# A planned recurrence and feed-forward kernel on one core: later loads planned as late, and part of the first group's up products in split passes

## The chip, the cores and the metric

The kernel runs on one core of one Trainium2 chip. The metric is device time in microseconds (us) of one execution, the median over runs. TensorE multiplies matrices, VectorE, ScalarE and GpSimd do elementwise work, SyncE issues the transfers between DRAM and the on-chip memory. Each engine works through its own instructions strictly in order. An instruction whose operand is not ready holds back all that stand behind it on its engine.

## The reference

What is computed is a recurrence over 768 steps for 4 batches and 8 heads of width 48, and then a two-layer product over the 3072 tokens that it gives:

```python
for t in range(S):                                  # B=4, H=8, S=768, D=48
    cur = np.einsum('bhd,bhe->bhde', u[None] * kt, vt)
    y[:, :, t] = np.einsum('bhd,bhde->bhe', rt, state + cur)
    state = wt[:, :, :, None] * state + np.einsum('bhd,bhe->bhde', kt, vt)
...
h = x @ w_in                                        # x: y as 3072 x 384; w_in: 384 x 2048
g = np.maximum(h, 0.0) + alpha * np.minimum(h, 0.0)
return g @ w_out                                    # w_out: 2048 x 384
```

All is fp32.

## The kernel before

The time axis is cut into 12 blocks of 64 steps, and the batches into two pairs, so there are 24 *chunks* (q = 0 to 23) of 128 tokens. Each chunk is loaded by SyncE in three or four transfers (`load`: wd, kr, rk, nv) and prepared on VectorE, GpSimd and ScalarE (`prep`: two scans of the decays wd, two products that scale the keys and queries kr, a sum cd, eight small scalings into at). TensorE then makes its scores, its outputs and the new state St (`scores`, `outputs`, L452), and a transposition (L498).

Three chunks make a *group* (g = 0 to 7) of 384 tokens. A group goes through the 16 *tiles* (j = 0 to 15, called tile 1 to tile 16 here) of the hidden width. For each tile there is an *up* product (`moe_up`, L669) into a bank, then L674 on ScalarE and L676 on VectorE for the activation `pos`, and, two tiles later, the *down* products (`moe_down`, L694) that add into the three accumulators op0 to op2. The program's names in the profile and in the order's rows carry running numbers (wf_81 is the first tile of wf, wf_96 the sixteenth in the kernel before).

There are two ways to multiply. Groups 1 to 7 split each operand into a high part in fp32r and the remainder, also in fp32r (x, wh and wl, gh and gl), and do three fp32r passes: nine instructions of 384 columns for an up product. Group 0 multiplies the unsplit fp32 operands (x_0, named xw in the rows, and wf): three fp32 instructions for an up product, each of which shows as two rows of TensorE. The splitting of a weight tile is `weight_parts`: ScalarE casts wf to wh (L650) and VectorE subtracts (L651, wl). Ahead of it `weight_tile` rebuilds a tile of weights from its 64-bit packing: one ScalarE instruction (L630) and three on VectorE (L632, L635, L639), the last of which writes wf.

The order of all engines' instructions is fixed when the program is built. `Plan.order` plays a list of operations with assumed durations and waits, and picks on each engine the ready one with the earliest due time. The due times come from tables of constants (FIRST, PLACE, PLACE_REST, AHEAD, ATT). For a transfer it assumes a landing DMA_LAT + lat after the issue. Where it sees TensorE idle ahead of the first use of op2, it puts in *fillers* (L818), products that nobody reads. Late in the program the inputs are loaded once more to be checked on ScalarE (`check_load`, L766, ScalarE lines L774, L783 and L784).

Ahead of each of groups 1 to 7, once its third chunk's x is split (L574, L585), four transfers (L606) move parts of x into place; the group's first up product waits for them.

## Time and profile before

| | us |
|---|---|
| median of 3 runs | 511.61 (507.61 to 512.86) |
| the profiled execution | 509.13 |
| its span, first to last instruction | 507.3 |
| TensorE busy in it | 494.3 |
| VectorE busy | 338.2 |
| ScalarE busy | 290.8 |
| GpSimd busy | 79.4 |

The profiled execution is one run of its own: 1.8 us of its time lie outside the span. Busy times of TensorE count pipelined instructions up to their modelled ends, so that the time one takes from the engine is read from one start to the next.

### The profile page before, as it was taken

The page shows a single profiled execution, that of the slowest core. Times are in us where ns is not written, and L with a number is a line of the kernel's source. Part 1 is how long each engine was busy: PE and PEld are TensorE (multiplying, and loading weights), DVE is VectorE, ACT ScalarE, POOL GpSimd, SP SyncE. Part 2 cuts the span into 40 slices and gives each one's busy share as a digit, 9 for nine tenths or more (in the row PEclk, how much of TensorE's full clock was granted, in tenths as well). Part 3 has the DMA queues.
Part 4 walks back from the last instruction along what each step waited for, and adds up shares of the span by engine and source line. Part 5 has one row for each costly group of instructions (what it writes and reads, how often), then busy time and mean ns, then how long its engine had stood idle before and what let it go on. Part 6 is the DMA issues. An engine that isn't in the chain of part 4 may idle for free.

```text
span 507.3 us, 13038 instructions
## 1 busy us (share of the span) xinstructions
PE 494.3 (97%) x5404; PEld 457.8 (90%) x5404; DVE 338.2 (67%) x602; ACT 290.8 (57%) x746; POOL 79.4 (16%) x103
## 2 busy tenths in 40 slices
PE   8999998999999999999999999999999999999994
PEld 8976664699999999999998999989999999999994
DVE  7999999999886656938377474945566344343331
ACT  5866485453454536457584656667677676553331
POOL 2111333350114010402014020220000000000000
PEclk9999999999999999999999999999999999999998
DMA  8966776550352302735175653746455531210001
GB/s 311 365 212 228 265 238 213 151 161 23 111 149 79 112 22 77 221 90 202 49 216 163 159 175 105 237 131 205 147 179 159 170 127 63 88 42 6 1 3 53
DMA packets 27109, 72.42 MB, mean 143 GB/s; under 512 B 3680, under 2 KB 8224, under 8 KB 27040
## 3 DMA queue, kind: packets, MB, share of 16 engines
q1 hardware_dynamic: 26656, 71.19, 43.9%
q8 instruction: 44, 0.72, 0.6%
q10 hardware_dynamic: 384, 0.30, 0.2%
q14 instruction: 25, 0.20, 0.1%
HBM read 64.70 MB, written 4.72 MB: 137 GB/s over the span
## 4 chain that ended last, share of the span: by engine, by line
PE 78%; DVE 12%; DMA 5%; issue 2%; SPq 1%; ACT 1%; DVEq 0%; ACTq 0%
PE bank L669 35%; PE op L694 33%; PE bank L452 7%; DMA raw<-in_wts_dram 2%; DVE cx L635 2%; DVE wf L639 2%; DVE suf L395 2%; DMA kr<-in_dmaj_dram 1%; PE bank L498 1%; DVE pos L676 1%; DVE kr L404 1%; DVE kr L407 1%; DVE cx L632 1%; PE bank L561 1%; DVE wd L401 1%
## 5 line engine op out<-in xcount | busy, mean ns | idle before, releaser
L669 PE MATMUL bank<-x,wh 128*128 128x384 f32 x672 | 191.7, 339 | 0.5 <-DMA x<-x 0.5
L674 ACT ACTIVATE pos<-bank,alpha_n 128x384 f32<-128x384 f32 (+1 forms) x133 | 75.3, 567 | 100.7 <-PE bank L669 100.3
L676 DVE SCALAR_TENSOR_TENSOR pos<-bank,pos 128x384 f32<-128x384 f32 (+1 forms) x133 | 71.3, 536 | 82.3 <-ACT pos L674 82.1
L669 PEld LDWEIGHTS bank<-x,wh 128*128 128x128 f32 x672 | 123.0, 188 | 2.5 <-ACT os L711 1.1
L694 PE MATMUL op<-wh,gh 128*128 128x384 f32 x336 | 113.3, 337 | 0.8 <-ACT gh L680 0.8
L694 PE MATMUL op<-wh,gl 128*128 128x384 f32 x336 | 112.8, 336 | 1.4 <-DVE gl L681 1.2
L694 PE MATMUL op<-wl,gh 128*128 128x384 f32 x336 | 112.5, 335 | 0.0
L669 PE MATMUL bank<-x,wl 128*128 128x384 f32 x336 | 112.4, 335 | 0.0
L681 DVE TENSOR_TENSOR gl<-pos,gh 128x384 fp32r<-128x384 f32 x112 | 68.3, 610 | 55.6 <-ACT gh L680 54.9
L680 ACT CAST gh<-pos 128x384 fp32r<-128x384 f32 x112 | 57.4, 512 | 51.4 <-DVE pos L676 51.2
L694 PEld LDWEIGHTS op<-wh,gl 128*128 128x128 f32 x336 | 63.1, 188 | 2.5 <-DVE gl L681 2.5
L694 PEld LDWEIGHTS op<-wh,gh 128*128 128x128 f32 x336 | 63.1, 188 | 1.4 <-ACT gh L680 1.4
L669 PEld LDWEIGHTS bank<-x,wl 128*128 128x128 f32 x336 | 63.1, 188 | 0.1
L694 PEld LDWEIGHTS op<-wl,gh 128*128 128x128 f32 x336 | 63.1, 188 | 0.0
L443 POOL TENSOR_TENSOR St<-St,pc_all 128x192 f32<-128x192 f32 x44 | 25.1, 589 | 232.5 <-DVE St L596 172.1
L433 ACT ACTIVATE at<-twin,cd 128x64 f32<-128x64 f32 x192 | 52.9, 340 | 2.4 <-DVE cd L428 1.9
L425 POOL TENSOR_TENSOR rk<-rk,u_bc 128x384 f32<-128x384 f32 x19 | 24.3, 1279 | 93.2 <-DMA rk<-in_nat_dram 50.5
L669 PE MATMUL bank<-xw,wf 128*128 128x384 f32 (+2 forms) x126 | 35.3, 418 | 1.8 <-DVE wf L639 1.7
L694 PE MATMUL op<-wf,pos 128*128 128x384 f32 x96 | 34.4, 489 | 0.0
L395 DVE TENSOR_TENSOR_SCAN suf<-wd,low 128x528 f32<-128x528 f32 x24 | 30.0, 1248 | 3.7 <-DMA wd<-in_dmaj_dram 3.7
L669 PEld LDWEIGHTS bank<-xw,wf 128*128 128x128 f32 x126 | 20.6, 190 | 12.5 <-DVE wf L639 2.9
L401 DVE TENSOR_TENSOR_SCAN wd<-wd,low 128x528 f32<-128x528 f32 x24 | 31.6, 1318 | 0.1
(81 smaller groups left out, 530.5 us busy)
## 6 DMA issues: line engine op xcount, KB each, us to landing
raw<-in_wts_dram SPq DMA_DIRECT2D x32, 768.0 KB, 4.7
kr<-in_dmaj_dram SPq DMA_DIRECT2D x24, 512.0 KB, 4.0
rk<-in_nat_dram SPq DMA_DIRECT2D x19, 384.0 KB, 3.4
wd<-in_dmaj_dram SPq DMA_DIRECT2D x24, 264.0 KB, 2.9
raw<-in_dmaj_dram SPq DMA_DIRECT2D x12, 528.0 KB, 4.0
nv<-in_nat_dram SPq DMA_DIRECT2D x24, 256.0 KB, 4.9
out_dram<-os SPq DMA_DIRECT2D x44, 96.0 KB, 2.2
x<-x SPq DMA_DIRECT2D x28, 72.0 KB, 4.2
```

The lines of the kernel that those rows point to most:

```text
L395: op("DVE", 1.17, lambda: nc.vector.tensor_tensor_scan(out=suf.ap[:, ::-1], data0=w.ap[:, ::-1], data1=low[:, ::-1], initial=0.0, op0=ALU. ...
L401: op("DVE", 1.17, lambda: nc.vector.tensor_tensor_scan(out=w.ap, data0=w.ap, data1=low, initial=0.0, op0=ALU.mult, op1=ALU.max), r=["low"] ...
L425: op("POOL", 1.0, lambda i=i: nc.gpsimd.tensor_tensor(out=rk.ap[:, 0:HD], in0=rk.ap[:, 0:HD], in1=u_bc if i == 0 else rk.ap[:, HD:], op=AL ...
L433: nc.scalar.activation(out=at.ap[:, o, p, :], in_=twin, func=AF.Copy, scale=cd.ap[:, o * NP + p:o * NP + p + 1])
L443: op("POOL", 0.6, lambda i=i: nc.gpsimd.tensor_tensor(out=St[b][:, i, :, 0:D], in0=St[b][:, i, :, 0:D], in1=pc_all[:, q, i::2].unsqueeze(2 ...
L452: nc.tensor.matmul(yb[q][i].ap[rows, cols], start=(i, rows.start) not in opened[q], stop=stop, skip_group_check=True, **kw)
L669: nc.tensor.matmul(hp.ap[:, ts], lhsT=a, rhs=b[:, k, ts], start=(i == 0), stop=(i == m - 1))
L674: op("ACT", 0.15 + 0.33 * share, lambda: nc.scalar.activation(out=pos.ap[:, ts], in_=hp.ap[:, ts], func=AF.Relu, scale=alpha_n[:, j:j + 1] ...
L676: op("DVE", 0.07 + 0.4 * share, lambda: nc.vector.scalar_tensor_tensor(out=pos.ap[:, ts], in0=hp.ap[:, ts], scalar=0.0, in1=pos.ap[:, ts], ...
L680: op("ACT", 0.43, lambda: nc.scalar.copy(out=gh.ap, in_=pos.ap), r=[pos], w=[gh])
L681: op("DVE", 0.47, lambda: nc.vector.tensor_tensor(out=gl.ap, in0=pos.ap, in1=gh.ap.bitcast(F32), op=ALU.subtract), r=[pos, gh], w=[gl], lo ...
L694: nc.tensor.matmul(ops_[s], lhsT=a.ap[:, ts], rhs=w, start=(j == 0 and i == 0), stop=(j == NF - 1 and i == len(todo) - 1))
```

## The change

Seven things change; the reference's result is computed in both.

1. In the planner, a transfer marked `kind` counts as landed LATE = 4.6 later than before for those that read it. Marked are the loads of chunks 6 to 23 and all check loads.
2. With UPS = 10, the up products of group 0 from tile 11 on take the three fp32r passes. For them the three chunks of x_0 are split once more into a ring tile `parted` (one ScalarE copy, one VectorE subtraction for each chunk), and the first halves of tiles 11 to 16 are split at once when they are rebuilt.
3. The weight tiles are kept in halves (up half 0, down half 1): the last rebuilding step and the splitting are two instructions of 384 columns where one of 768 stood. The ring cx has two places in place of one.
4. JOIN = 6: chunks 4, 5 and 6 get their scores in an operation of their own, not joined to the chunk before.
5. The due times are new (FIRST, PLACE, PLACE_REST, EDGE, AHEAD 14.2, ATT 1.23).
6. The unused constant `minus` and the path LO_BY_PE go.
7. In groups 0 to 6 the middle accumulator is copied out by ScalarE, not by VectorE.

```diff
-ATT = 0.5
-JOIN = 3
-AHEAD = 8.8
+ATT = 1.23
+JOIN = 6
+AHEAD = 14.2
...
+LATE = 4.6
+LATE_FROM = 6
+UPS = 10
...
                     dma = max(dma, end + DMA_LAT) + o.lat
-                    end = dma
+                    end = dma + (LATE if o.kind else 0.0)
...
+        def w_low(j, i):
+            slot = j if i == 0 and j >= UPS else (j - 1) % (NF + 1)
+            return half(wl, j, i, slot, F32R)
...
-        r_cx = ring("cx", [P, 2 * DM], 1, I32)
+        r_cx = ring("cx", [P, 2 * DM], 2, I32)
...
-            natural = q >= U_BY_PE
-            op("SP", 0.4, lambda: nc.sync.dma_start(out=w.ap, in_=dmaj[q, :, 0:SC]), w=[w], lat=0.75)
+            natural, far = q >= U_BY_PE, q >= LATE_FROM
+            op("SP", 0.4, lambda: nc.sync.dma_start(out=w.ap, in_=dmaj[q, :, 0:SC]), w=[w], lat=0.75, kind=far)
...
+            if g == 0 and UPS < NF:
+                part = lambda l: parted.ap[:, l, 0:KT, ss]
+                op("ACT", 0.42, lambda: nc.scalar.copy(out=part(0), in_=x_0[:, :, ss]), ...
+                op("DVE", 0.47, lambda: nc.vector.tensor_tensor(
+                    out=part(1), in0=x_0[:, :, ss], in1=part(0).bitcast(F32), op=ALU.subtract), ...
...
-                op("DVE", 0.07 + 0.4 * n, lambda x=x, w0=w0, full=full: nc.vector.tensor_tensor(
-                    out=full().bitcast(I32), in0=x(), in1=w0(), op=ALU.add), r=[k0, cx], w=keys("wf"), lock=True,
-                   due=tile_due[j] - AHEAD)
+                for i in range(i0, i1):
+                    early = i == 0 and j >= UPS
+                    op("DVE", 0.47, lambda cx=cx, fi=fi, full=full: nc.vector.tensor_tensor(
+                        out=full().bitcast(I32), in0=cx.ap[:, fi], in1=raw.ap[:, fi, 0], op=ALU.add), ...
+                    if early:
+                        parting(j, i, full, [cx, (cx, i)])
+        def parting(j, i, full, source):
+            op("ACT", 0.41, lambda: nc.scalar.copy(out=wh[:, j, i, :], in_=full()), r=source, w=[("wh", j, i)])
+            op("DVE", 0.47, lambda: nc.vector.tensor_tensor(
+                out=w_low(j, i), in0=full(), in1=wh[:, j, i, :].bitcast(F32), op=ALU.subtract), ...
...
         def moe_up(n, g, s0, s1, j):
-            x = xs[g]
+            parts = g > 0 or j >= UPS
+            x = xs[g] if g > 0 else parted
...
-                if s == 1 or last and s == GS - 1:
+                if last and s > 0:
```

The table of due times sets the order anew on every engine. Three places matter for what follows. TensorE, near 14 us, after the scores of the first two chunks; L498 and L507 are transpositions, L561 and L571 spread a chunk's outputs, L418 and L427 make a chunk's sums, L818 and L832 are fillers. Before:

```order
L498 MATMUL bank_75<-ident,kr_119 128x112 x4
L818 MATMUL op_74<-os_144 128x128 x2
L561 MATMUL bank_78<-os_144,os_145 128x64 x3
L561 MATMUL bank_79<-os_144,os_145 128x64 x3
L818 MATMUL op_74<-os_144 128x128
```

After:

```order
L427 MATMUL bank_75<-u_dm,rk_138 128x2 x4
L571 MATMUL bank_78<-os_160,os_161 128x64 x3
L571 MATMUL bank_79<-os_160,os_161 128x64 x3
L507 MATMUL bank_75<-ident,kr_136 128x112 x4
L832 MATMUL op_74<-os_160 128x128 x5
```

There are five fillers where three stood, and the sums of chunk 2 (rk_138) have moved ahead of the spreading; over the whole program the fillers are 25 in place of 16.

VectorE, at the last tile of group 0; wf_96 and cx_132 to wl_0_111 are tile 16, x_131 and x_149 the remainder of group 1's x, bank_77 and so on the chunk's outputs. Before:

```order
L632 TENSOR_SCALAR cx_115<-raw_114 128x768
L651 TENSOR_TENSOR wl_1014<-wf_82,wh 128x768
L635 SCALAR_TENSOR_TENSOR cx_115<-raw_114,cx_115 128x768
L651 TENSOR_TENSOR wl_1019<-wf_83,wh 128x768
L639 ISA wf_96<-raw_114,cx_115 128x1536
L676 SCALAR_TENSOR_TENSOR pos_136<-bank_79,pos_136 128x384
L651 TENSOR_TENSOR wl_1096<-wf_84,wh 128x768
L395 SCALAR_TENSOR_TENSOR suf_126<-wd_117,low 128x528
L585 TENSOR_TENSOR x_131<-bank_77,x_131 128x4x64
L585 TENSOR_TENSOR x_131<-bank_78,x_131 128x4x64
```

After:

```order
L638 TENSOR_SCALAR cx_132<-raw_130 128x768
L658 TENSOR_TENSOR wl_0_109<-cx_131,wh 128x384
L641 SCALAR_TENSOR_TENSOR cx_132<-raw_130,cx_132 128x768
L658 TENSOR_TENSOR wl_1_1158<-wf_1_82,wh 128x384
L648 ISA cx_132<-raw_130,cx_132 128x768
L648 ISA wf_1_112<-raw_130,cx_132 128x768
L586 TENSOR_TENSOR x_149<-bank_75,x_149 128x4x64
L586 TENSOR_TENSOR x_149<-bank_78,x_149 128x4x64
L658 TENSOR_TENSOR wl_0_111<-cx_132,wh 128x384
```

The remainder of x of group 1's third chunk, which stood behind the last tile, stands ahead of its last piece now, and the tile ends with a subtraction (L658) that waits for a ScalarE copy.

VectorE, at chunk 17's keys (kr_120 before, kr_137 after), whose transfer the trace shows late. Before:

```order
L676 SCALAR_TENSOR_TENSOR pos_137<-bank_77,pos_137 128x384
L483 COPY_PREDICATED at_130<-mask,bank_78 128x256
L398 RECIPROCAL low<-suf_126 128x8
L428 TENSOR_REDUCE cd_128<-rk_122 128x8
L681 TENSOR_TENSOR gl_143<-pos_137,gh_140 128x384
L401 SCALAR_TENSOR_TENSOR wd_117<-wd_117,low 128x528
L404 TENSOR_TENSOR kr_120<-kr_120,suf_126 128x512
L676 SCALAR_TENSOR_TENSOR pos_135<-bank_79,pos_135 128x384
```

After:

```order
L413 TENSOR_TENSOR kr_136<-kr_136,suf_143 128x512
L416 TENSOR_TENSOR kr_136<-kr_136,wd_133 128x512
L695 TENSOR_TENSOR gl_159<-pos_151,gh_156 128x384
L404 SCALAR_TENSOR_TENSOR suf_143<-wd_134,low 128x528
L690 SCALAR_TENSOR_TENSOR pos_153<-bank_77,pos_153 128x384
L407 RECIPROCAL low<-suf_143 128x8
L437 TENSOR_REDUCE cd_144<-rk_138 128x8
L410 SCALAR_TENSOR_TENSOR wd_134<-wd_134,low 128x528
L695 TENSOR_TENSOR gl_157<-pos_153,gh_154 128x384
L690 SCALAR_TENSOR_TENSOR pos_152<-bank_79,pos_152 128x384
L413 TENSOR_TENSOR kr_137<-kr_137,suf_143 128x512
```

Ahead of the first product on the late keys (L404 before, L413 after) there stand two more activations (pos) and one more remainder (gl) that do not need them.

## Rows read from the trace of the kernel before

**Rows 1.** The page: busy time, then slices of 12.7 us (VectorE, granted clock).

```profile
PE 494.3 (97%) x5404; PEld 457.8 (90%) x5404; DVE 338.2 (67%) x602; ACT 290.8 (57%) x746; POOL 79.4 (16%) x103
...
DVE  7999999999886656938377474945566344343331
...
PEclk9999999999999999999999999999999999999998
```

**Rows 2.** Busy us of each engine (executed instructions), clock, DMA, in 76 to 96 us.

```profile
76.00:96.00 20.00, 18.29 (x181) 10.96 (x180) 20.00 (x29) 11.00 (x28) 6.35 (x6) 1.00 0.58 196
```

**Rows 3.** Waits of TensorE: line, releaser, us in total, times, longest.

```profile
PE bank L669 <- DVE wf L639: 1.7, 2, 1.0
```

**Rows 4.** TensorE timeline, end of the first group: start, us, instruction, idle before.

```profile
76.82 2.10 PE L669 MATMUL bank<-xw,wf 128*128 128x384 f32 x6
78.76 2.10 PE L694 MATMUL op<-wf,pos 128*128 128x384 f32 x6
81.59 2.20 PE L669 MATMUL bank<-xw,wf 128*128 128x384 f32 x6 [0.74 <-DVE wf L639]
83.63 2.74 PE L694 MATMUL op<-wf,pos 128*128 128x384 f32 x8
87.35 2.20 PE L669 MATMUL bank<-xw,wf 128*128 128x384 f32 x6 [0.97 <-DVE wf L639]
...
93.02 0.43 PE L452 MATMUL bank<-kr,St 64*64 64x64 f32 x16
...
93.84 2.20 PE L669 MATMUL bank<-xw,wf 128*128 128x384 f32 x6
95.88 4.03 PE L694 MATMUL op<-wf,pos 128*128 128x384 f32 x12
100.44 0.41 PE L669 MATMUL bank<-x,wh 128*128 128x384 f32 x1 [0.52 <-DMA x<-x]
```

**Rows 5.** The chain of work, second group: start, us, what.

```profile
116.99 1.56 PE bank L669 x9
```

**Rows 6.** TensorE timeline, the first fillers (L818) and what follows.

```profile
5.69 0.61 PE L818 MATMUL op<-os 128*128 128x128 f32 x4
6.14 0.95 PE L418 MATMUL bank<-u_dm,rk 128*128 128x2 f32 x8
```

**Rows 7.** VectorE timeline, 91 to 96 us: the first group's last weight tile, the second group's x.

```profile
91.22 0.94 DVE L639 CUSTOM_DVE_ANT_0 wf<-raw,cx 128x1536 uint16<-128x1536 uint16 x1
92.08 0.55 DVE L676 SCALAR_TENSOR_TENSOR pos<-bank,pos 128x384 f32<-128x384 f32 x1
92.55 1.29 DVE L651 TENSOR_TENSOR wl<-wf,wh 128x768 fp32r<-128x768 f32 x1
93.77 1.24 DVE L395 TENSOR_TENSOR_SCAN suf<-wd,low 128x528 f32<-128x528 f32 x1
94.94 0.72 DVE L585 TENSOR_TENSOR x<-bank,x 128x256 fp32r<-128x256 f32 x2
```

**Rows 8.** The chain of work at the two late transfers: issue, us to landing.

```profile
259.62 7.54 DMA kr<-in_dmaj_dram
...
325.15 6.71 DMA raw<-in_wts_dram
```

**Rows 9.** VectorE and ScalarE timelines: who waited for those two transfers.

```profile
267.18 0.69 DVE L404 TENSOR_TENSOR kr<-kr,suf 128x512 f32<-128x512 f32 x1 [2.24 <-DMA kr<-in_dmaj_dram]
...
331.88 0.54 ACT L783 ACTIVATE raw<-raw 128x384 f32<-128x384 f32 x1 [3.30 <-DMA raw<-in_wts_dram]
```

**Rows 10.** TensorE timeline at the same two places.

```profile
268.94 0.44 PE L694 MATMUL op<-wh,gh 128*128 128x384 f32 x1
270.61 0.44 PE L694 MATMUL op<-wh,gl 128*128 128x384 f32 x1 [1.23 <-DVE gl L681]
...
331.69 0.34 PE L694 MATMUL op<-wl,gh 128*128 128x384 f32 x1
332.88 0.44 PE L694 MATMUL op<-wh,gh 128*128 128x384 f32 x1 [0.85 <-ACT gh L680]
```

## What was predicted

> **What bounds the kernel now.** I read the page's slices first, then the busy times by stretch, then TensorE's waits and the timelines at the places that these name. TensorE is busy 494.3 us of a span of 507.3, and its granted clock reads 9 in every slice but the last [rows 1], so it runs at its upper level of 2.4 GHz and no part of the change has a lower clock to win back or much idleness to remove. Almost all of the time is work. VectorE shows 9 in the slices from 13 to 127 us and falls to 3 to 6 later. The start, that is the attention of the first chunks, the rebuilding of the weights and group 0, has two engines full at once: from 76 to 96 us VectorE is busy 20.00 us of 20, ScalarE only 11.00, and TensorE 18.29 [rows 2].
>
> TensorE's real gaps after the first microseconds are few. Twice an up product waits for the last rebuilding step of its weight tile, 1.7 us in all [rows 3]; the timeline shows them at 81.59 (0.74) and 87.35 (0.97), and one for the moved parts of x at 100.44 (0.52) [rows 4]. Later there are two, both behind a late transfer. A load of keys took 7.54 us from 259.62 on, a check load 6.71 us from 325.15 on [rows 8]. The first kept VectorE waiting 2.24 us, the second ScalarE 3.30 us [rows 9], although neither product was wanted soon: in the queues behind them stood activations that TensorE did want, and it went idle at 268.94 and 331.69 [rows 10].
>
> So the change can gain in two places: at those two late transfers, and in the first 100 us, where it takes work from TensorE but gives work to the engine that is full.
>
> **The change part by part.**
>
> *Later landings in the plan.* Nothing is added to any engine; the order moves. The plan of before had the keys land 2.0 + 1.5 = 3.5 us after the issue, at 263.1; VectorE asked for them at 267.18 - 2.24 = 264.94. With 4.6 us more the plan holds them back to 8.1 us, over the 7.54 of the row; for the check load it is 2.0 + 2.0 + 4.6 = 8.6 against 6.71. The new order does what that asks: two activations, two remainders and the two products of the chunk before now stand between that chunk's x and the late keys, where one activation and one remainder stood. Each of the two more counts 0.47 us (the step from 92.08 to 92.55 in [rows 7]), each product of 512 columns 0.63 by the same rate: 2.2 us, as much as the 2.24 of the wait. What goes is TensorE's lost time: 268.94 to 270.61 less one step of 0.17 (a ninth of the 1.56 in [rows 5]) is 1.50 us, 331.69 to 332.88 less the same is 1.02. Sum 2.5 us. What is late next is the preparation of the following chunk, which has several units of 3.1 us ahead of its use. Bounds: 2.5 us of gain, and 0 if another wait takes their place. I take 2.5, because both transfers were shorter than what is now planned.
>
> The Trainium skill would say there was nothing to plan for: "DMA: Bandwidth & Descriptors", section "Anatomy of one DMA — SWDGE (gpsimd) path", fits 2.0 us plus bytes over 436 per ns, an estimate of 3.2 us for the 512 KB of keys. They would have landed at 262.8, ahead of VectorE's question, this term would be 0 and the result 509.3. That fit is for the GpSimd path, and the row here shows 7.54; the measurement decides.
>
> *Up products in three passes.* Six tiles change. An fp32 up product takes 78.76 - 76.82 = 1.94 us of TensorE [rows 4], nine fp32r instructions take 1.56 [rows 5]: 6 x 0.38 = 2.3 us less work.
>
> *Separate scores.* Chunks 4, 5 and 6 leave and enter the attention once more each. The up product behind attention takes 95.88 - 93.84 = 2.04 us, 0.10 more than the 1.94 without. I take as much again on the way in and inside, so 0.3 per chunk as an estimate, 0.9 in all, with 0.3 and 0.9 as ends.
>
> *Fillers.* Nine more. Two of them take 6.14 - 5.69 = 0.45 us [rows 6], so nine take 2.0. Where TensorE would stand idle they cost nothing; where it is late they cost all. They lie before 35 us. Ends 0 and 2.0.
>
> *VectorE until tile 16.* This is where the change adds. Counted in the two orders up to the last piece of tile 16:
> - The 16 rebuilding steps L639 (0.86, from 91.22 to 92.08 [rows 7]) become 32 of 384 columns (0.47): +1.3 us.
> - Three subtractions of 768 columns (0.86 like those) become four of 384, and six early ones are added: 10 x 0.47 - 3 x 0.86 = +2.1.
> - The remainders of x_0 for three chunks: +1.4.
> - One more sum (0.45) and two more remainders of x (0.66, from the row at 94.94): +1.1.
> - Chunk 6's preparation, two scans of 1.17 (93.77 to 94.94) and two products of 512 columns (0.63 each), moves behind: -3.6.
>
> Sum: +2.3 us. The last tile was ready at 92.08; it is ready at 94.4 then, and its up product starts there rather than at 93.84. Then 1.56 for it and 1.94 for three downs: 97.9. But group 1 also needs its x. Its remainder stands just ahead of the last piece, so at about 93.9, and from there the trace took 100.44 - 95.66 = 4.8 us for issuing and landing the moves: 98.7. At 100.44 the old order had one down left of group 0, the new one has three (2 x 0.67 more) and chunk 6's scores to do (93.02 to 93.84, 0.8). So 98.7 + 1.3 + 0.8 = 100.8 against 100.44: **+0.4 us**. The 2.3 us less of TensorE are used up in waiting for VectorE.
>
> The other end is a TensorE that waits for nothing: -2.3 (passes), -2.2 (the three waits of [rows 4]), +0.9 (scores), and fillers at 0 to 2.0, that is -3.6 to -1.6. I take +0.4, because VectorE had no idle time at all there [rows 2].
>
> The Trainium skill has a rule that speaks against halves: "Perfetto Trace Analysis", section "Optimizing Scalar/DVE Operations", puts an overhead of about 60 ns on each VectorE instruction on SBUF and advises larger operations on a saturated engine. By that the 16 extra rebuilding steps cost an estimated 1.0 us; the rows' 0.47 against half of 0.86 give 1.3.
>
> *The rest* costs nothing that I can find: the accumulators' copies go to ScalarE, at 11 of 20 even in the full stretch; cx's second place only loosens; the split of the remaining 26 halves continues in group 1, where VectorE has slack again.
>
> **Sum.** The profiled execution took 509.13: 509.13 - 2.5 + 0.4 = **507.0 us**. The median of the three runs is 2.5 us above it, the fastest 1.5 below; late transfers fall differently in each run, which is what this change is made against, so I leave the forecast at the profiled one's sum.
>
> **The rivals.**
> *A, TensorE sets the end of group 0.* If VectorE's order is better packed (tiles are due 14.2 us ahead rather than 8.8), the waits at 81.59 and 87.35 go and the 2.3 us count: 506.6 less 1.6 to 3.6, middle 504.0. For it: VectorE's last tile was ready 1.8 us ahead of its use (92.08 against 93.84). Against: that engine gets the 2.3 us more.
> *B, the change doesn't do what it says.* A transfer later than planned, or another one, stalls the queues elsewhere; the late term is 0 and the start as forecast: 509.5. For it: the planner moves order only, an engine still blocks in order. Against: both margins cover the rows.
> *C, slower: VectorE waits for ScalarE in the tiles 11 to 16.* The early subtraction needs the cast of the same half by ScalarE, and between the two VectorE has only two instructions, some 0.9 us. If ScalarE, busy with scalings and activations, comes 0.9 us later than that, six tiles lose 5.4 us, all on the full engine: 507.0 + 5.4 = 512.4. It decides once ScalarE's queue lags VectorE by over 0.9 us; at 0.4 the result is still no slower than before. For it: VectorE is full, so nothing is made up. Against: ScalarE's 11.00 of 20.
>
> **How the numbers follow.** Forecast 0.45, A 0.23, B 0.17, C 0.15. The predicted time is 507.0. The range, 503.0 to 512.0, reaches from A's lower part to C's; about 0.1 lies above and 0.08 below. About 1%, 5.1 us, is what a measurement of this kernel can tell from no change. Faster by over 1% means under 504.0 by the profiled execution and under 506.5 by the median; A gives 0.18 of that, and of the forecast a third, for the case that runs of before lie at the median: 0.15. So 0.33. Slower by over 1%: two thirds of C, 0.1. Within: 0.57.
>
> **What would show it.** In the changed profile: no wait of VectorE for kr or of ScalarE for raw that reaches TensorE between 210 and 430 us (late term); up products of tiles 11 to 16 at 1.56 us; group 1's first up product near 98.7, with a wait for x or for the last tile's subtraction (my start); no such wait and a start before 97 would be A; VectorE idle behind ScalarE casts (L657) between 65 and 95 us would be C. I am wrong if the time from 130 us on grows, which I count as equal, or if fillers push TensorE past VectorE before 60 us.

## The result, and the profile after

The changed kernel takes 512.01 us in the median of 22 executions (509.39 to 514.37) where the kernel before, timed beside it, takes 511.11 (506.42 to 514.63): a ratio of 1.0059, 95% interval 1.0039 to 1.0080. By that ratio, which goes by the fast executions of each kernel (the two medians lie 0.9 us apart), it is slower by about 3 us, where 507.0 was forecast. Its profiled execution took 513.14 us over a span of 511.4, 4.0 more than that of before.

The page first: busy time, then VectorE and the granted clock in 40 slices of 12.8 us.

```profile
PE 497.8 (97%) x5440; PEld 463.4 (91%) x5440; DVE 351.7 (69%) x630; ACT 297.5 (58%) x771; POOL 72.0 (14%) x103
...
DVE  6999999899999465874769556886547343433332
...
PEclk9999999999999999999999999999999999999998
```

Against [rows 1] VectorE is busy 13.5 us more. Work added explains under 1 us of that: 1.3 each for the two kinds of halves and 1.4 for the remainders of x_0, by the prediction's prices, less 3.3 for the seven copies of accumulators that went to ScalarE (0.47 each). The rest is instructions that take longer than the same ones did before. TensorE too is busy 3.5 us more, where the passes were to save 2.3; by the steps from start to start the nine fillers more take 2.1 of that.

Busy microseconds (and instructions) of each engine in three stretches, then clock, DMA share and GB/s; the first row answers to [rows 2].

```profile
76.00:96.00 20.00, 18.65 (x210) 13.11 (x203) 18.30 (x34) 11.49 (x28) 3.22 (x3) 1.00 0.67 224
250.00:300.00 50.00, 50.00 (x636) 48.19 (x635) 33.97 (x61) 32.92 (x87) 7.72 (x10) 1.00 0.51 150
300.00:350.00 50.00, 50.00 (x639) 48.75 (x639) 37.15 (x64) 33.47 (x92) 10.44 (x12) 1.00 0.58 174
```

TensorE is busy for all of 250 to 350 us: the waits of [rows 10] are gone, as forecast. But VectorE, full in [rows 2], now has holes in its fullest stretch. What TensorE waits for (line, releaser, us in total, times, longest) shows where the time went; [rows 3] had one of these rows.

```profile
PE op L708 <- DVE gl L695: 1.7, 4, 0.5
PE bank L683 <- DVE wl L658: 1.7, 3, 0.7
PE bank L683 <- DVE wf L648: 1.2, 1, 1.2
```

Four down products (L708) wait for gl, the lower part of an activation: new waits against the profile of before, all between 157 and 222 us, at the ends of groups 1 and 2. Three up products of the split tiles wait for the lower part of a weight. The last of the six, TensorE:

```profile
97.93 0.44 PE L683 MATMUL bank<-x,wh 128*128 128x384 f32 x1
98.99 0.45 PE L683 MATMUL bank<-x,wl 128*128 128x384 f32 x1 [0.62 <-DVE wl L658]
...
100.49 2.10 PE L708 MATMUL op<-wf,pos 128*128 128x384 f32 x6
```

It takes 100.49 - 97.93 = 2.56 us. The six take 1.67 to 2.62, 13.6 in all, where the forecast had 1.56 each, 9.4.

The end of group 0, VectorE then GpSimd then TensorE (start, us, instruction, idle before it):

```profile
83.50 0.55 DVE L658 TENSOR_TENSOR wl<-wf,wh 128x384 fp32r<-128x384 f32 x1
83.96 1.37 DVE L648 CUSTOM_DVE_ANT_0 cx<-raw,cx 128x768 uint16<-128x768 uint16 x1
85.25 1.36 DVE L648 CUSTOM_DVE_ANT_0 wf<-raw,cx 128x768 uint16<-128x768 uint16 x1
...
94.47 1.06 DVE L658 TENSOR_TENSOR wl<-cx,wh 128x384 fp32r<-128x384 f32 x1 [1.30 <-ACT wh L657]
...
97.73 0.74 DVE L586 TENSOR_TENSOR x<-bank,x 128x256 fp32r<-128x256 f32 x2
```

```profile
83.89 1.02 POOL L434 TENSOR_TENSOR rk<-rk,u_bc 128x384 f32<-128x384 f32 x1 [8.87 <-DMA rk<-in_nat_dram]
84.99 1.20 POOL L434 TENSOR_TENSOR rk<-rk 128x384 f32<-128x384 f32 x1
```

```profile
102.76 0.41 PE L683 MATMUL bank<-x,wh 128*128 128x384 f32 x1 [0.17 <-DMA x<-x]
```

Two rebuilding steps of 0.55 us take 1.37 and 1.36, exactly beside GpSimd's two products on rk, which started when their transfer landed. The second of them frees the place for the last weight tile: the step ends at 86.61, the load is issued at 86.68 and lands 5.9 us later, ScalarE waits for it, and VectorE waits for a cast behind it (the 1.30). The last remainder of x stands at 97.73. The x moves are issued at 98.50, not 93.9 as forecast, and group 1's first up product stands at 102.76, not 98.7. SyncE, before and after:

```profile
95.69 2.90 SPq L606 DMA_DIRECT2D x<-x  x4
```

```profile
98.50 2.63 SPq L614 DMA_DIRECT2D x<-x  x4
```

The same pattern once more in group 1, VectorE, GpSimd and TensorE:

```profile
158.88 0.68 DVE L413 TENSOR_TENSOR kr<-kr,suf 128x512 f32<-128x512 f32 x1
159.47 1.50 DVE L416 TENSOR_TENSOR kr<-kr,wd 128x512 f32<-128x512 f32 x1
160.90 1.36 DVE L695 TENSOR_TENSOR gl<-pos,gh 128x384 fp32r<-128x384 f32 x1
```

```profile
159.24 1.19 POOL L434 TENSOR_TENSOR rk<-rk,u_bc 128x384 f32<-128x384 f32 x1 [5.09 <-DMA rk<-in_nat_dram]
160.50 1.35 POOL L434 TENSOR_TENSOR rk<-rk 128x384 f32<-128x384 f32 x1
```

```profile
162.31 0.44 PE L708 MATMUL op<-wh,gl 128*128 128x384 f32 x1 [0.35 <-DVE gl L695]
```

The Trainium skill has this in "SBUF — State Buffer", section "Who interferes with whom": VectorE and GpSimd share one pair of ports, and a VectorE instruction with two SBUF inputs contends with a GpSimd instruction that reads SBUF. The trace agrees: L648, L416 and L695 read two SBUF tiles each, and in these rows each takes 0.8 us more. What is lost looks like the rest of the product that is met: the product of 83.89 ends at 84.91 and L648 at 85.33, the next at 86.19 and 86.61, that of 160.50 at 161.85 and L695 at 162.26, each 0.41 or 0.42 later.

To size it: VectorE's steps (start to start) from the first instruction to the issue of group 1's x moves, each against the lower quartile of the steps of its form, with the idle time that rows name counted apart. How the quartile is taken moves some 0.5 us between the second and the last column.

| | x moves issued | undisturbed steps | idle | over the steps |
|---|---|---|---|---|
| before | 95.69 | 84.3 | 0.7 | 7.0 |
| changed | 98.50 | 83.5 | 2.1 | 9.3 |

The work until there did not grow at all (-0.8). Disturbed steps (+2.3), idle time (+1.4, nearly all of it the 1.30 in the row at 94.47) and a start 0.3 us later made the 2.8 us; the changed kernel's sum is 0.4 too long, as its moves are issued ahead of the end of the last step.

Over the whole span a reckoning of the same kind gives 306.6 us of undisturbed steps before and 306.9 after. The steps that overlap one of GpSimd's two products are 14.1 us over theirs before and 25.7 after.

TensorE's granted clock bears on the times. Of the 103 executions of the kernel before that were timed beside the variants of the experiments, 38 have a mean granted clock under 0.9925 and a median of 512.0 us, the other 65 one of 507.7. Of the changed kernel's 22 one is under it, and the others have 511.9. So with the clock up the loss is 4.2 us, near the 4.0 between the two profiles (clocks 0.996 and 0.997).

### The profile page after: what moved, and what is told of

Same layout as the page of the kernel before. It is cut to its first block, busy times and chain, and to the rows that moved or that the text cites. A ratio compares the mean times of both kernels' runs of the same rounds, so it can differ in the third digit from the quotient of the medians.

```text
span 511.4 us, 13156 instructions
## 1 busy us (share of the span) xinstructions
PE 497.8 (97%) x5440; PEld 463.4 (91%) x5440; DVE 351.7 (69%) x630; ACT 297.5 (58%) x771; POOL 72.0 (14%) x103
## 4 chain that ended last, share of the span: by engine, by line
PE 79%; DVE 14%; DMA 4%; issue 2%; ACT 1%; SPq 0%; POOL 0%; ACTq 0%; DVEq 0%; POOLq 0%
PE bank L683 34%; PE op L708 33%; PE bank L461 8%; DMA raw<-in_wts_dram 3%; DVE wf L648 2%; DVE cx L641 2%; DVE pos L690 1%; PE bank L507 1%; DVE cx L638 1%; PE op L832 1%; DVE gl L695 1%; PE bank L737 1%; DVE kr L416 1%; DVE wd L410 1%; DVE suf L404 1%
## 5 line engine op out<-in xcount | busy, mean ns | idle before, releaser
L683 PE MATMUL bank<-x,wh 128*128 128x384 f32 x708 | 203.2, 341 | 0.2 <-DMA x<-x 0.2
L690 DVE SCALAR_TENSOR_TENSOR pos<-bank,pos 128x384 f32<-128x384 f32 (+1 forms) x133 | 71.5, 538 | 93.5 <-ACT pos L688 93.1
L683 PEld LDWEIGHTS bank<-x,wh 128*128 128x128 f32 x708 | 129.6, 188 | 3.3 <-issue 1.0
L683 PE MATMUL bank<-x,wl 128*128 128x384 f32 x354 | 119.0, 336 | 1.8 <-DVE wl L658 1.7
L708 PE MATMUL op<-wh,gl 128*128 128x384 f32 x336 | 113.2, 337 | 1.8 <-DVE gl L695 1.7
L708 PE MATMUL op<-wh,gh 128*128 128x384 f32 x336 | 113.4, 337 | 0.0
L708 PE MATMUL op<-wl,gh 128*128 128x384 f32 x336 | 112.5, 335 | 0.0
L695 DVE TENSOR_TENSOR gl<-pos,gh 128x384 fp32r<-128x384 f32 x112 | 69.1, 617 | 43.4 <-ACT gh L694 43.0
L683 PEld LDWEIGHTS bank<-x,wl 128*128 128x128 f32 x354 | 66.5, 188 | 3.6 <-DVE wl L658 3.5
L708 PEld LDWEIGHTS op<-wh,gl 128*128 128x128 f32 x336 | 63.1, 188 | 4.2 <-DVE gl L695 3.8
L708 PEld LDWEIGHTS op<-wh,gh 128*128 128x128 f32 x336 | 63.1, 188 | 0.3
L708 PEld LDWEIGHTS op<-wl,gh 128*128 128x128 f32 x336 | 63.1, 188 | 0.0
L452 POOL TENSOR_TENSOR St<-St,pc_all 128x192 f32<-128x192 f32 x44 | 22.7, 537 | 241.9 <-DVE St L604 151.8
L708 PE MATMUL op<-wf,pos 128*128 128x384 f32 x96 | 35.0, 491 | 0.0
L434 POOL TENSOR_TENSOR rk<-rk,u_bc 128x384 f32<-128x384 f32 x19 | 20.7, 1091 | 93.8 <-DMA rk<-in_nat_dram 93.8
L404 DVE TENSOR_TENSOR_SCAN suf<-wd,low 128x528 f32<-128x528 f32 x24 | 31.1, 1296 | 4.0 <-POOL os L328 4.0
L434 POOL TENSOR_TENSOR rk<-rk 128x384 f32<-128x384 f32 x19 | 25.5, 1342 | 1.3
L708 PEld LDWEIGHTS op<-wf,pos 128*128 128x128 f32 x96 | 17.5, 190 | 8.8
## 6 DMA issues: line engine op xcount, KB each, us to landing
kr<-in_dmaj_dram SPq DMA_DIRECT2D x24, 512.0 KB, 4.3
```

The source lines that it names most:

```text
L404: op("DVE", 1.17, lambda: nc.vector.tensor_tensor_scan(out=suf.ap[:, ::-1], data0=w.ap[:, ::-1], data1=low[:, ::-1], initial=0.0, op0=ALU. ...
L434: op("POOL", 1.0, lambda i=i: nc.gpsimd.tensor_tensor(out=rk.ap[:, 0:HD], in0=rk.ap[:, 0:HD], in1=u_bc if i == 0 else rk.ap[:, HD:], op=AL ...
L452: op("POOL", 0.6, lambda i=i: nc.gpsimd.tensor_tensor(out=St[b][:, i, :, 0:D], in0=St[b][:, i, :, 0:D], in1=pc_all[:, q, i::2].unsqueeze(2 ...
L683: nc.tensor.matmul(hp.ap[:, ts], lhsT=a, rhs=b[:, k, ts], start=(i == 0), stop=(i == m - 1))
L690: op("DVE", 0.07 + 0.4 * share, lambda: nc.vector.scalar_tensor_tensor(out=pos.ap[:, ts], in0=hp.ap[:, ts], scalar=0.0, in1=pos.ap[:, ts], ...
L695: op("DVE", 0.47, lambda: nc.vector.tensor_tensor(out=gl.ap, in0=pos.ap, in1=gh.ap.bitcast(F32), op=ALU.subtract), r=[pos, gh], w=[gl], lo ...
```

## The experiments

Ratios are to the kernel before, timed beside on the same chip; 95% intervals in brackets.

**1. One part each.** Four kernels took the change apart by its constants.

The kernel before with late planning alone:

```
+LATE = 4.6
+LATE_FROM = 6
-                    end = dma
+                    end = dma + (LATE if o.kind else 0.0)
...
```

> The kernel before with the late planning alone (4.6 us more for the loads of chunks from the seventh on and for the check's loads; tables, whole weight tiles and up products as before). Theory T, the late planning is worth what the traces of before and after show between 250 and 367 us (2.9 us): 508.4 us, ratio 0.994 to 0.995, no PE wait at 260 to 340 us that follows a late kr or raw transfer, and the prologue to group 1's first up product at 100.4 us as before within 0.5 us. Rival L, the late planning is itself what costs 1.8 to 3 us in groups 1 to 3, because it moves other operations: 511 us, ratio 0.998 to 1.002, with new waits of down products for the VectorE parts of their activations at 150 to 225 us.

518.17 us, 1.0212 [1.0148, 1.0275]. Neither theory. All six executions have a mean clock under 0.9925. The x moves come at 98.77, and then a hole stands at the start of group 1 (waits of TensorE):

```profile
PE bank L671 <- DVE pos L678: 5.5, 1, 5.5
PE op L696 <- DVE gl L683: 2.4, 4, 0.9
```

Behind it stands ScalarE, whose copy of an accumulator waits for an output transfer, with the activation queued behind:

```profile
107.52 0.48 ACT L713 COPY os<-op 128x384 f32<-128x384 f32 x1 [3.19 <-DMA out_dram<-os]
```

While TensorE stands idle the granted clock falls: it reads 0.50, 1.2 GHz, from 108 to 114 us.

The changed kernel without late planning:

```
-LATE = 4.6
+LATE = 0.0
```

> The changed kernel with the late planning taken out (extra time 0 us), everything else as changed. Theory T: the loss stays and the gain goes, 512.0 + 2.9 = 514.9 us, ratio 1.006 to 1.009, with two PE waits of 1.0 to 1.5 us behind late transfers at 255 to 340 us back. Rival L (late planning costs in groups 1 to 3 what it gains later): 511 to 512 us, ratio 1.000 to 1.003, and no waits of down products for the lower parts of their activations at 150 to 225 us.

513.34 us, 1.0090 [1.0051, 1.0129]. Between the theories, and its interval overlaps that of the changed kernel: late planning is worth 0.3% there, with an uncertainty of about 0.4. No wait behind a late transfer came back at TensorE between 255 and 340 us, so the changed order avoids them without it.

The changed kernel with whole up products, and with the tables of before:

```
-UPS = 10
+UPS = 16
```

> The changed kernel with all up products of group 0 as one fp32 product again, so without the early halves, without the parted copy of x and with tiles 11 to 16 as before; tables and late planning as changed. Theory S (the split up products' VectorE work beside GpSimd's, and the short time left after the last weight tile, hold back group 1): group 1's first up product at 100 to 101 instead of 102.8 us and the whole at 509.5 to 510.5 us, ratio 0.995 to 0.998. Theory T2 (the loss comes from the tables, which start the first up products 2.7 to 3.2 us later and push VectorE's weight work to the end): group 1's first up product stays at 102.5 to 104 us and the whole at 511.5 to 513 us, ratio 1.001 to 1.005.

519.09 us, 1.0206 [1.0139, 1.0272], neither theory: the x moves at 106.49, VectorE idle 5.5 us before them.

```
-AHEAD = 14.2
+AHEAD = 8.8
...
-FIRST = [(0, 1, 0, 28.3), (0, 1, 1, 7.2), ...
+FIRST = [(0, 1, 0, 35.4), (1, 2, 0, 40.2), ...
```

> The changed kernel with all its tables (places of the first chunks, pieces and preparations, lead of the weights, joined pieces) set back to those of before; split up products and late planning stay. Theory T2 (tables): first up product near 18.5 us instead of 21.2, group 1's first up near 100 us and the whole at 507.5 to 509.5 us, ratio 0.992 to 0.997. Theory S (split up products): first up product near 18.5 us, but the end of group 0 as late as in the changed kernel, 511 to 513 us, ratio 1.000 to 1.004.

513.49 us, 1.0093 [1.0057, 1.0130]. The first up product is back at 17.94 us, the x moves are not (100.57): of theory T2 its first half, for the rest theory S. All four are slower than before, two by 2%. The parts are no terms that add: each constant makes the replay lay all of the first 100 us anew, and the tables fit one set of constants only. From here on every kernel keeps the built order and changes one thing in it.

**2. GpSimd's products made small.**

```
-    out=rk.ap[:, 0:HD], in0=rk.ap[:, 0:HD], in1=u_bc if i == 0 else rk.ap[:, HD:], op=ALU.mult),
+    out=rk.ap[:, 0:D], in0=rk.ap[:, 0:D], in1=u_bc[:, 0:D] if i == 0 else rk.ap[:, HD:HD + D], op=ALU.mult),
```

> The changed kernel with GpSimd's two products of each chunk from the sixth on cut from 384 to 48 columns (7/8 of the current token's diagonal sums are left out for these chunks); every instruction of every engine stays in its place. In the changed kernel VectorE's instructions until the x move of group 1 take 9.4 us more than their undisturbed steps, in the kernel before 7.0 us. Theory G (GpSimd's products beside VectorE are where the changed kernel loses): these 9.4 us fall to 3 to 4, the x move comes 3 to 5 us sooner (near 94 us), the waits of down products for the lower parts at 157 to 221 us (1.7 us) go, and the whole takes 505.5 to 508 us, ratio 0.990 to 0.994. Rival O (order: the last weight tile lands late, VectorE idles 1.3 us for ScalarE's cast, work stands behind other work): the x move comes no more than 1.5 us sooner and the whole takes 510 to 511.5 us, ratio 0.998 to 1.002.

> The kernel before with the same cut of GpSimd's products to 48 columns (the same sums left out), in an unchanged order. Theory G: VectorE's 7.0 us over the undisturbed steps fall to 3 to 4, the x move comes 2 to 3 us sooner than at 95.7 us, and the whole takes 508 to 509.5 us, ratio 0.994 to 0.997, so that it and the changed kernel with the same cut differ by less than 1 us in the prologue. Rival O: 510 to 511.5 us, ratio 0.998 to 1.001, and the distance to the changed kernel with the same cut stays 3 us.

Changed kernel: 506.16 us, 0.9935 [0.9904, 0.9965]; kernel before: 506.31 us, 0.9944 [0.9910, 0.9979]. Theory G holds, though neither x move comes as early as it said (95.33 and 94.11). The difference between the two kernels is gone in the medians; with the clock up 1.0 us is left (506.2 in all 12 executions of the changed kernel, 505.2 in 9 of 12 of the kernel before). Over the undisturbed steps of the table VectorE spends 2.6 us (for 9.3) and 3.1 us (for 7.0). Over the whole span the steps that overlap a product are 2.0 us over theirs (for 25.7) and 1.4 (for 14.1). The same rows as above, of the changed kernel with the small products:

```profile
82.96 0.65 DVE L658 TENSOR_TENSOR wl<-wf,wh 128x384 fp32r<-128x384 f32 x1
83.53 0.64 DVE L648 CUSTOM_DVE_ANT_0 cx<-raw,cx 128x768 uint16<-128x768 uint16 x1
84.09 0.55 DVE L648 CUSTOM_DVE_ANT_0 wf<-raw,cx 128x768 uint16<-128x768 uint16 x1
...
91.72 0.56 DVE L658 TENSOR_TENSOR wl<-cx,wh 128x384 fp32r<-128x384 f32 x1 [0.61 <-ACT wh L657]
...
94.56 0.74 DVE L586 TENSOR_TENSOR x<-bank,x 128x256 fp32r<-128x256 f32 x2
```

The two steps are back at 0.55 to 0.64, the wait for ScalarE's cast is halved, and the x remainder stands 3.2 us earlier. (Some of what VectorE saves it idles elsewhere: 5.8 us in all for 2.1.) No wait for gl is left in the trace, in either kernel. A shorter product is also ready sooner, but no row of either kernel's trace, with the whole products, has VectorE waiting for one; experiment 6 takes the products from GpSimd without making them shorter.

**3. The early and the late chunks apart.** The same cut, in the changed kernel, for some chunks. The texts of the runs count chunks from one: 6 to 11 are q = 5 to 10. The other run has `q >= 11` in the first line:

```
+                    n = D if q < 11 else HD
...
+                        out=rk.ap[:, 0:n], in0=rk.ap[:, 0:n], in1=u_bc[:, 0:n] if i == 0 else rk.ap[:, HD:HD + n], op=ALU.mult),
```

> The changed kernel with GpSimd's products cut to 48 of 384 columns for chunks 6 to 11 alone, those whose products fall before 113 us (7/8 of their current token's diagonal sums are left out). With all of them cut the changed kernel fell from 512.0 to 506.2 us, 4.6 of the 5.8 us by 162 us in the traces. Theory P (the products cost in the prologue): the x move at 95 to 96 us, the waits of down products at 157 to 221 us still there, 507.5 to 509 us, ratio 0.995 to 0.998. Rival S (they cost in the steady groups, by those waits): 510.5 to 511.5 us, ratio 1.001 to 1.003.

> The changed kernel with the products cut for chunks 12 to 24 alone (7/8 of their diagonal sums left out). Theory P: the prologue as in the changed kernel (x move 97.5 to 100 us), the waits at 157 to 221 us gone, 510 to 511 us, ratio 1.000 to 1.003. Rival S: 507.5 to 509 us, ratio 0.995 to 0.998.

Early: 509.06 us, 0.9998 [0.9966, 1.0030], x moves at 95.34, three waits for gl left (1.4 us). Late: 509.57 us, 1.0005 [0.9972, 1.0039], x moves at 96.59, no wait for gl. Both theories are half right: of 1.24% in all the early chunks carry 0.61 and the late ones 0.54, 3 us each, with an uncertainty of about 0.4 each. The late variant leaves the early chunks as they are in the changed kernel, and yet its x moves come 1.9 us sooner than there: the place of the x moves in one profile says less than the medians.

**4. The late transfers by themselves.** In the kernel before two moves in the built order:

```
+        order = behind(order, [named["DVE", "kr", 17], named["DVE", "wkr", 17], named["DVE", "suf", 18]], named["DVE", "gl", 66])
+        order = behind(order, [named["ACT", "sq", 1, 0]], named["ACT", "gh", 83])
```

behind takes instructions out of their place, with those that depend on them, and puts them after the last one named.

> The kernel before with two moves in its order and nothing else: on VectorE three instructions of chunks 18 and 19 (two products on kr and the next scan) stand behind the lower part of the activation that they held up at 267 us, and on ScalarE one square of the check stands behind the cast that it held up at 332 us. Theory T (the late transfers cost TensorE 1.50 and 1.02 us, 2.9 us with the row behind them, and a planner that knew of them would save just that): both PE waits go, 508.4 to 509 us, ratio 0.994 to 0.996. Rival W (the work that waited for the transfer now holds up the next activation, as in the runs with late planning, which show new waits of 0.5 to 0.9 us in the same stretch): one or two waits of 0.4 to 0.9 us in their place within 10 us, 510 to 511 us, ratio 0.998 to 1.000.

508.70 us, 1.0004 [0.9964, 1.0044]: no gain, nor with the clock up (507.8 in 7 executions, 507.7 in 19 of the kernel before beside them). VectorE, then TensorE, at the first place:

```profile
267.15 0.56 DVE L701 TENSOR_TENSOR gl<-pos,gh 128x384 fp32r<-128x384 f32 x1 [0.58 <-ACT gh L700]
...
271.13 1.51 DVE L421 TENSOR_TENSOR_SCAN wd<-wd,low 128x528 f32<-128x528 f32 x1
272.57 1.29 DVE L701 TENSOR_TENSOR gl<-pos,gh 128x384 fp32r<-128x384 f32 x1
```

```profile
273.91 0.44 PE L714 MATMUL op<-wh,gl 128*128 128x384 f32 x1 [1.15 <-DVE gl L701]
```

Rival W, with an addition: the wait of 1.23 [rows 10] is replaced by one of 1.15 an activation later. The work that had waited for the keys now stands ahead of the next gl, and that gl itself takes 1.29 instead of 0.56 beside a GpSimd product. The wait at the check load is gone.

**5. Both kernels once more,** unchanged, one profile each.

> The kernel before, unchanged, profiled once more. Its timed executions fall into two groups by the mean granted clock: 0.995 to 0.999 with a median of 507.7 us, and 0.985 to 0.992 with a median of 511.7 us (19 and 16 of 35). Theory K: an execution of the first group shows late transfers that cost TensorE less than the 2.5 us of the first profile (0 to 1.5 us between 255 and 340 us); one of the second shows a stretch at 1.2 GHz of 5 to 6 us, within the first 130 us and behind a stretch in which TensorE waited, and is 3 to 5 us late from there on. Rival: the waits at 268.9 and 331.7 us are there again with 1.5 and 1.0 us, and the second group differs by something spread over the span.

> The kernel before, unchanged, once more (it takes two or more executions to see one of each group): as for the first repeat.

> The changed kernel, unchanged, profiled once more; 21 of its 22 executions had a clock of 0.993 to 0.998 and a median of 511.9 us. Theory K: no stretch at 1.2 GHz longer than 2 us after the first 20 us, the x move at 97 to 99 us, and waits of down products for the lower parts of 0.35 to 0.5 us at 150 to 225 us in the same four places, 1 to 2 us in sum. Rival: these waits are chance, and stand at other places or are absent.

The kernel before took 512.89 us (clock 0.991) and 506.79 (0.998), one of each group; the changed kernel 514.34. The first repeat, in stretches of 2 us:

```profile
16.00:18.00 2.00, 0.67 (x9) 0.42 (x9) 2.00 (x5) 1.49 (x5) 0.00 (x0) 1.00 1.01 390
...
20.00:22.00 2.00, 2.00 (x13) 2.00 (x12) 0.28 (x3) 1.29 (x6) 0.00 (x0) 0.55 0.99 375
22.00:24.00 2.00, 2.00 (x11) 2.00 (x11) 2.00 (x4) 0.81 (x4) 1.93 (x2) 0.50 0.84 251
24.00:26.00 2.00, 2.00 (x7) 1.39 (x7) 1.15 (x3) 2.00 (x8) 0.00 (x0) 0.50 0.39 160
26.00:28.00 2.00, 2.00 (x16) 2.00 (x15) 0.28 (x2) 0.79 (x3) 0.00 (x0) 0.74 0.51 135
```

TensorE is idle for 1.33 us in 16 to 18, and the clock then stands at 1.2 GHz from about 20.2 to 27 us. VectorE, which needs TensorE's results there, idles 5.5 us before the x moves (100.25), and the kernel is some 4.9 us late from there on (group 1's first up product at 105.27 for the 100.44 of [rows 4]). The other repeat has no such stretch. That much is theory K. But the idle time does not bring the low clock each time; the kernel before with small products has as much of it, and its clock stays up:

```profile
16.00:18.00 2.00, 0.69 (x8) 0.44 (x8) 2.00 (x5) 1.54 (x5) 0.00 (x0) 1.00 1.05 395
20.00:22.00 2.00, 2.00 (x20) 2.00 (x19) 0.81 (x5) 1.74 (x8) 0.46 (x1) 1.00 0.98 372
```

The late transfers of [rows 8] are in neither as they were: the keys kept VectorE waiting 0.78 and 1.36 us, the check load ScalarE 1.53 and 1.42, and TensorE lost in this stretch 0.97 us (at 277.96) and 1.4 us (at 268.72 and 272.67); at the check load nothing. The first repeat also has two short waits for gl in groups 1 and 2 (0.19 and 0.31). The changed kernel's repeat has three of the four waits for gl (1.4 us); of theory K it misses two things, with 3.4 us at 1.2 GHz (18.0 to 21.4) and the x moves at 100.33. The steps that overlap a product are 16.1, 14.4 and 23.5 us over theirs in the three, near the 14.1 and 25.7 of the first profiles.

**6. The products on VectorE.** GpSimd's two products done by VectorE right ahead of the sum L437: first in the changed kernel for all chunks, then in the kernel before, with the two moves of experiment 4, for chunks 12 to 24.

```
-                    op("POOL", 1.0, lambda i=i: nc.gpsimd.tensor_tensor(
...
+                    op("POOL", 1.0, lambda: None, r=["u"], w=[rk], lock=True)
+                def sum_rk():
+                    for i in range(2):
+                        nc.vector.tensor_tensor(
...
```

> The changed kernel with GpSimd's two products of each chunk done by VectorE itself, right ahead of the sum that reads them; nothing else moves. VectorE gets 2 x 0.47 = 0.94 us more for a chunk and loses what the products cost it beside it (about 0.8 us on an instruction that runs beside one). Theory G: the prologue comes out even or up to 2 us shorter (5 or 6 chunks x 0.94 = 5 us added, 6 us taken), the inflated rows of 1.3 to 1.8 us are gone, the whole takes 509.5 to 512 us, ratio 0.997 to 1.001. Rival O (the added work lies on VectorE's path and the products cost it little): the x move 4 to 5 us later, the whole 515 to 517 us, ratio 1.007 to 1.012.

511.36 us, 1.0047 [1.0012, 1.0083]: even, as theory G has it. VectorE's undisturbed steps before the x moves rise by 4.8 us, what is over them falls by 7.3 (2.0 for 9.3), and the x moves come at 95.21.

> The kernel before with the two moves and, for chunks 12 to 24 alone, GpSimd's two products done by VectorE right ahead of the sum that reads them (all of the output is computed). In the steady groups VectorE is busy for 58 to 67% of the time. If the products' cost to VectorE is what delays activations there, this gains what the kernel before with small products gained behind 130 us, some 1 to 2 us: 508 to 509 us, ratio 0.995 to 0.998. Rival: 0.94 us more of VectorE's work for a chunk delays the activations just as much: 509.5 to 511 us, ratio 0.999 to 1.003.

516.08 us, 1.0113 [1.0058, 1.0169] (514.9 in the three of six executions with the clock up). The rival, and more: 0.94 us of VectorE's own work in a row ahead of a gl holds it up just as a disturbed step does.

```profile
PE op L719 <- DVE gl L706: 3.9, 9, 0.6
```

**7. The fillers.** The kernel before with 23 fillers for 16, and the changed kernel with 15 for 25:

```
-FILL, FILL_MIN = 0.24, 0.35
+FILL, FILL_MIN = 0.16, 0.35
```

```
-FILL, FILL_MIN = 0.24, 0.35
+FILL, FILL_MIN = 0.45, 0.35
```

> The kernel before with 21 fillers in place of 14 (the planned time of one set from 0.24 to 0.16 us; nothing else moves). In the two repeats of the kernel before a granted clock of 1.2 GHz stood from 20.2 to 27 us in one and nowhere in the other; the changed kernel, with 19 fillers, had one in 18 to 21.3 us in one of two. Theory F (the fillers keep TensorE busier ahead of its first products and so the clock up): the executions with a mean clock under 0.9925 (16 of 35 of the kernel before, 1 of 22 of the changed kernel) fall to 2 in 12 or fewer, the lowest time stays near 505.5 us and the median comes to 508 us, ratio 0.995 to 0.998. Rival: the share stays at 4 to 6 of 12 and the ratio at 0.999 to 1.001; then it is the changed order of the first chunks, not the fillers, that kept the clock up.

> The changed kernel with 15 fillers in place of 25 (the planned time of one set from 0.24 to 0.45 us; nothing else moves). Counted in the built order, the kernel before has 16 and its variant with more has 23 (not 14 and 21, as the expectation of that run has it); that variant had no execution of 12 under a mean clock of 0.9925, where the kernel before had 8 of 29, and took 0.1% longer all the same. Theory F2 (the fillers keep the clock up at 18 to 28 us, and cost about as much as they save, since the first products wait behind them): 4 or more of 12 executions under 0.9925, those above it at a median of 509.5 to 511 us, 1 to 2 us under the changed kernel's 511.9 us, and the whole at a ratio of 1.002 to 1.006. Rival: clock and time stay as in the changed kernel (0 or 1 of 12 under 0.9925, median of the others within 0.7 us of 511.9 us).

With more: 510.75 us, 1.0012 [0.9976, 1.0047]; none of 12 executions under 0.9925 (8 of 29 of the kernel before beside it), yet those 12 have a median 2.9 us above the others of before: theory F has the clock right and the time wrong. With fewer: 512.11 us, 1.0070 [1.0032, 1.0108], 2 of 12 under it; the profile is one of the two, at 1.2 GHz from about 13 to 23 us. So ten fillers less neither give the changed kernel time nor clearly bring the low clock; theory F2 falls.

## Why the prediction was wrong

**The bound was read rightly.** VectorE sets the end of group 0 in both kernels; rival A needed a TensorE that waits for nothing.

**The step that failed is the sum "VectorE until tile 16", +2.3 us, within the prologue's +0.4.** It counted instructions at undisturbed durations and let the disturbance of the old order stand. The counted work was nearly right: -0.8 us until the x moves, where the prediction had them 1.8 us sooner (93.9 for 95.69). What it left out was 2.3 us of VectorE steps that the new order puts beside GpSimd's products, and 1.4 us of idle time, most of it at the last weight tile, whose load waited for a place that disturbed steps freed late. The x moves thus came 4.6 us after the forecast, the first up product of group 1 4.1 us after it. By the prediction's own reckoning (102.76 + 1.3 + 0.8 against 100.44) the prologue cost 4.4 us and not 0.4. The experiments show the disturbance as the cause: with the products cut for the early chunks alone the kernel is 0.61% faster, and without them on GpSimd the x moves come at 95.21 although VectorE has 4.8 us more to do.

**"The time from 130 us on, which I count as equal" grew.** The four new waits of TensorE for gl, 1.7 us, go with the late chunks' products; these cost the changed kernel 0.54%. The prediction named this as what would make it wrong, and had no price for it.

**The late term, -2.5 us, was mis-sized.** In the profiles it came out (the waits are gone), but the 2.5 us were one execution's: two more show 1.0 and 1.4 us lost in that stretch, part of it behind a gl that takes 1.3 us beside a product, and the two moves that undo just these waits gain 0.0% (interval +-0.4%). Rival B's "the late term is 0" was the better number, though not because transfers land in time. The Trainium skill's fit in "DMA: Bandwidth & Descriptors", section "Anatomy of one DMA — SWDGE (gpsimd) path", weighed in the prediction, gave 0 as well (509.5 by its sum, not the 509.3 there), by keys that VectorE never waits for; in all three profiles of the kernel before it does, 0.78 to 2.24 us.

**The passes saved nothing that the traces show.** The six products took 13.6 us and 12.9 in the repeat, where six fp32 products of 1.94 take 11.6: in the first profile five of the six stand still after their first instruction, three of them for 0.46 to 0.66 us by rows that name the lower part of the weight. The prediction let the 2.3 us be used up in waiting, so its sum doesn't rest on them.

**Fillers, 0 to 2.0 us:** nothing in the experiments speaks against 0 for them in the changed kernel, though they take 2.1 us of TensorE. Rival C's 512.4 lies next to the result, by chance: VectorE waited for the casts 1.30 us, not 5.4.

**Summed up:** GpSimd's products cost the kernel before 0.56% and the changed kernel 1.24%. The difference, 0.68% with an uncertainty of about 0.5, covers the loss of 0.59%. With the clock up it is 3.2 us of the loss of 4.2 (511.9 to 506.2 against 507.7 to 505.2). So the products are most of the loss; whether the last microsecond is noise, or the rest of the change, the runs don't tell.

**What stays open:** why TensorE stands idle at 16 to 18 us in some executions of the kernel before (the rows name no releaser there), why the clock falls behind it in some of these and not in others, and what in the changed kernel mostly keeps the clock from falling as long behind it. A version faster than both that computes everything was not found.

## What to carry to other kernels

When two engines contend, a planner that keeps them apart in planned time does not keep them apart on the chip: an engine with little to do starts when its transfer lands. Look at each instruction of the full engine that takes longer than its form does elsewhere, and at what ran beside it, before counting a reordering as free.

A stall read from one profile has the size of one execution. Before it is a term of a sum, look for it in a second one, and ask what the queue behind it does once it is gone: here the next activation waited as long.

Constants that feed one replay are no independent parts; to tell their effects apart, keep the built order and change one instruction's size, place or engine.

## What was not expected of the hardware

- A GpSimd product of 384 columns takes 1.0 us alone, mostly 1.2 to 2.0 beside VectorE, and 2.65 once (before, at 50.24). A VectorE instruction with two SBUF inputs that it meets takes up to 0.8 us longer: 0.55 became 1.37, a scan of 1.25 became 1.51 to 2.09. One with a single SBUF input is held up too, L638, whose 0.55 became 1.29. An activation (pos, L690), which reads its other operand from a bank, keeps its 0.55 beside a product (0.56 at 111.01).

```profile
44.01 1.29 DVE L638 TENSOR_SCALAR cx<-raw 128x768 int32<-128x768 int32 x1
```

```profile
43.89 1.00 POOL L434 TENSOR_TENSOR rk<-rk,u_bc 128x384 f32<-128x384 f32 x1 [15.92 <-DMA rk<-in_nat_dram]
```

- One idle stretch of 1.3 us of TensorE at 16 to 18 us was followed, 2 us later, by nearly 7 us at 1.2 GHz, and the kernel was 4.9 us late from there on, since VectorE then waited for TensorE on the path; another, as long, was followed by none. Over a third of the executions of the kernel before (38 of 103) have so low a mean clock.
